# A mixed-attention kernel: another plan table, output tokens turned back in pairs, a separate bank for the fourth key chunk and two queues for the last outputs

## The chip, the cores and the metric

The kernel runs on one core of a Trainium2 chip. The core has a matrix engine (TensorE, PE in the profile, with its weight loads as PEld), a vector engine (VectorE, DVE), an engine for functions of one operand (ScalarE, ACT), a general one (GpSimd, POOL) and SyncE (SP), which here issues DMAs. Each engine works through its own list of instructions in order, and semaphores hold the lists together. On-chip data lies in SBUF (128 partitions) and matrix results in PSUM, whose eight banks hold 512 float32 per partition each.

The metric is the device time of one execution in microseconds, as the median of several runs.

## What is computed

Two attentions over the same input are mixed by a gate. A is full softmax attention over 2,048 tokens with 32 heads of 20 channels; B looks at eight earlier tokens, two apart. Everything is bf16 at the interfaces.

```python
x = A_x                                             # 1 x 2048 x 640
g = sigmoid((x * gate_w).sum(-1, keepdims=True))
# A: q, k, v = split(x @ A_wqkv); per head
a = softmax(q @ k.T * 20 ** -0.5) @ v               # 2048 x 2048 scores per head
a = concat_heads(a) @ A_wo
# B: the same with its own weights; for each token only the keys at pos - 0, 2, ..., 14
b = concat_heads(o_B) @ B_wo
return g * a + (1 - g) * b
```

Most of the work is A: 32 heads of 2,048 x 2,048 scores, each with an exponential.

## The kernel before

**Tiling.** Queries are cut into four columns of 512 tokens (`qc`), heads into eight quads of four (`q`). A pair is a group; the 32 groups run in the order of `GROUPS`. In a group there are 16 blocks of 128 keys times four heads, so 64 score blocks of 128 keys x 512 queries, and 2,048 in all. A head's score block is one matrix product of 32 rows of `kT` and `qT` (20 channels, a bound, padding), so four heads share the partitions.

**The main loop.** `next_tile` takes two or three score blocks as a tile. `qk` (L1508) computes them into one of two triple banks, `score[0]` and `score[1]`, in turn. `exp` (L1531) is one exponential on ACT over the tile, into one of five `ebuf`. `pv` (L1576) multiplies the results with the values `vA` and accumulates the four heads of a quad in `obank`. So the score matmuls of tile s wait until the exponential of tile s-2 has read its bank. The third bank of each triple (`side[1]`, `side[2]`) can instead serve other work; `side[0]` always does. Those three are the side banks.

**Rides.** With a tile of two, a third score block may ride on DVE: L1521 turns the scores into integers that read as powers of two, L797 adds three shifts, and `vS` (made by POOL, L789) holds weighted values, so that four products of such blocks approximate the exponential. This takes blocks off ACT.

**The side work.** All else (projections of Q, K and V, the gate, attention B, and the fold, which is the last product with both output weights) is written as generators. They ask for a side bank, for PE time up to a limit, or for DVE. All their matmuls go through `mm_group` (L558), which cuts weights into pieces of 32 columns. `filler` (L1597) puts matmuls without use into gaps of PE.

**The order.** It is all made when the program is built. A planner keeps a model of when each engine is free; at each tile it grants side work until the earlier exponential's planned end plus `SLACK`. The table `PLAN` sets 18 numbers (`SLACK`, what a ride may wait for, priorities, the filler threshold and so on) from given tiles on. The chip only follows the resulting lists.

**Normalising.** When a group is done, `gen_norm` turns `obank` by 32 x 32 blocks (L759), takes the reciprocal of the denominators (L763), multiplies them with the gate (L765) and the outputs with both (L770, on POOL; on DVE in the last group), and turns the bf16 result back (L772) into `oN[1]`. DMAs spread it into `oTd`, whose columns are tokens; the fold uses 32 tokens at a time as weights.

**Head.** The first key quad is projected in four chunks (`k_first`, L1247) which take `side[0]` and `obank` in turn; each is measured by DVE (L1261) and copied to `kT` by ACT (L1268). The first query projection goes to `side[1]`, is turned into absolute values (L1323), a bound is added to it (L1326), and DVE writes `qT[0]` (L1331).

**Tail.** `gen_prefold` and `gen_prefold2` compute the last query column's fold for all but the last quad. Then `tail` (L1057) adds the last quad's part, ACT (L1076) and DVE (L1070, L1079) copy the results to SBUF, and SP issues four DMAs of 128 rows (L1084).

Of the kernel before, what the change touches and what calls it, by code (L numbers as in the profile page):

```python
# [14 lines left out]
P = 128  # L15
# [35 lines left out]
    0: ((0.36, 0.81), 0.32, 2.5, 6.6, 0.49, -1.0, -0.1, 11.8, 7.0, 7.2, 0.52, 0.47, 4.4, 4.44, 0.0, 0.85, 2, 0.0),  # L51
    10: ((0.41, 0.67), 0.29, 2.5, 6.6, 0.49, -1.0, -0.32, 10.6, 6.7, 7.2, 0.52, 0.61, 4.4, 4.44, 0.0, 0.85, 2, 0.0),
    30: ((0.3, 0.64), 0.32, 2.5, 2.5, 0.49, -1.0, -0.1, 11.8, 7.0, 6.95, 0.47, 0.5, 4.97, 4.0, 0.0, 0.85, 2, 0.0),
    40: ((0.42, 0.67), 0.29, 2.5, 6.6, 0.49, -1.0, -0.32, 10.6, 6.7, 7.2, 0.52, 0.61, 4.4, 4.44, 0.0, 0.85, 2, 0),
    70: ((0.41, 0.67), 0.29, 2.5, 2.5, 0.83, -1.02, -0.32, 10.6, 5.5, 7.2, 0.42, 0.61, 5.71, 4.44, -0.04, 0.85, 3, 0.0),
    80: ((0.42, 0.67), 0.29, 5.5, 6.6, 0.49, -1.0, -0.32, 10.6, 6.7, 7.2, 0.52, 0.48, 4.4, 4.44, 0.12, 0.85, 2, 0),
    90: ((0.42, 0.67), 0.05, 2.5, 6.6, 0.49, -1.0, -0.32, 10.6, 6.7, 7.2, 0.52, 0.61, 4.4, 4.44, 0.0, 0.6, 2, 0),
    110: ((0.3, 0.64), 0.32, 2.5, 1.0, 0.49, -1.0, -0.1, 11.8, 7.0, 7.2, 0.4, 0.47, 4.77, 3.55, -0.02, 0.85, 2, 0.0),
    120: ((0.3, 0.61), 0.32, 2.5, 6.3, 0.49, -1.0, -0.1, 10.63, 7.0, 7.2, 0.4, 0.56, 4.29, 4.0, 0.0, 0.85, 2, 1),
    130: ((0.3, 0.61), 0.28, 2.5, 6.3, 0.62, -1.0, -0.1, 10.63, 7.0, 7.2, 0.39, 0.56, 4.29, 4.0, 0.0, 0.85, 2, -3),  # L60
    140: ((0.3, 0.61), 0.22, 2.5, 5.5, 0.4, -1.0, 0.01, 9.77, 7.0, 7.2, 0.33, 0.21, 4.29, 4.0, 0.0, 0.85, 2, 0.0),
    150: ((0.3, 0.64), 0.32, 2.5, 2.5, 0.49, -1.0, -0.35, 11.8, 7.0, 7.2, 0.52, 0.47, 4.4, 4.0, 0.1, 0.85, 2, 0.0),
    190: ((0.3, 0.64), 0.32, 1.0, 2.5, 0.49, -1.0, -0.1, 11.8, 7.0, 7.2, 0.55, 0.47, 4.56, 4.0, 0.0, 0.85, 2, 0.0),
    200: ((0.3, 0.64), 0.32, 1.0, 2.5, 0.49, -0.57, 0.17, 11.8, 7.0, 7.2, 0.55, 0.47, 4.56, 4.0, 0.04, 0.85, 2, 0.0),
    210: ((0.3, 0.64), 0.32, 2.5, 2.5, 0.49, 0.26, 0.1, 11.8, 4.5, 11.1, 0.56, 0.32, 4.97, 4.0, -0.25, 0.85, 2, -3),
    230: ((0.3, 0.64), 0.32, 2.5, 2.5, 0.49, 0.05, -0.54, 11.8, 6.7, 11.1, 0.56, 0.47, 5.29, 2.82, -0.48, 0.85, 2, -3),
    240: ((0.3, 0.64), 0.32, 1.0, 6.3, 0.49, -0.85, -0.1, 11.39, 6.7, 11.1, 0.56, 0.27, 4.97, 4.0, -0.25, 0.85, 2, -3),
    260: ((0.3, 0.64), 0.32, 1.0, 6.3, 0.49, -0.34, -0.1, 11.39, 6.7, 10.86, 0.56, 0.27, 4.97, 4.0, 0.08, 0.85, 2, -3),
    290: ((0.3, 0.64), 0.32, 1.0, 6.3, 0.49, -0.34, -0.1, 11.39, 4.5, 10.86, 0.56, 0.27, 4.97, 4.0, 0.08, 0.85, 2, -3),
    300: ((0.3, 0.64), 0.32, 1.0, 6.3, 0.49, -0.34, -0.1, 11.39, 4.5, 10.86, 0.56, 0.27, 6.29, 4.0, 0.05, 0.85, 2, -3),  # L70
    320: ((0.3, 0.64), 0.27, 1.0, 6.3, 0.49, -0.83, -0.1, 11.39, 4.5, 10.86, 0.69, 0.23, 5.37, 4.0, 0.05, 0.61, 2, -3),
    330: ((0.3, 0.64), 0.27, 1.0, 6.3, 0.49, -0.72, -0.1, 11.39, 4.5, 7.69, 0.69, 0.23, 5.37, 4.0, 0.05, 0.61, 2, -3),
    340: ((0.3, 0.64), 0.14, 1.0, 6.3, 0.49, -1.05, 0.17, 11.39, 6.7, 10.63, 0.3, 0.34, 5.37, 4.43, 0.05, 0.61, 2, -3),
    350: ((0.3, 0.64), 0.16, 1.0, 6.3, 0.49, -0.25, -0.1, 8.61, 6.7, 10.86, 0.56, 0.27, 4.97, 4.0, 0.08, 0.85, 2, -3),
    360: ((0.3, 0.64), 0.27, 1.0, 5.5, 0.7, -0.83, -0.1, 12.93, 4.5, 11.67, 0.69, 0.23, 5.37, 4.0, 0.05, 0.61, 2, -3),
    390: ((0.3, 0.64), 0.27, 1.0, 6.3, 0.7, -0.83, -0.1, 12.93, 7.0, 10.86, 0.69, 0.23, 5.37, 4.0, 0.2, 0.61, 2, -3),
    400: ((0.3, 0.64), 0.27, 1.0, 6.3, 0.7, -0.83, -0.1, 12.93, 7.0, 9.69, 0.69, 0.23, 5.37, 1.85, 0.2, 0.6, 2, -3),
    420: ((0.3, 0.64), 0.27, 1.0, 6.3, 0.7, -0.83, -0.07, 12.93, 4.5, 10.86, 0.5, 0.23, 5.37, 4.0, 0.1, 0.61, 2, -3),
    430: ((0.3, 0.64), 0.27, 1.0, 6.3, 0.7, -0.83, -0.07, 12.93, 6.2, 10.86, 0.5, 0.23, 5.37, 4.0, 0.1, 0.61, 2, -3),
    440: ((0.3, 0.64), 0.27, 1.0, 6.3, 0.7, -0.83, -0.07, 12.93, 4.5, 10.86, 0.5, 0.23, 5.64, 4.45, 0.1, 0.75, 2, -3),  # L80
    460: ((0.3, 0.64), 0.27, 1.0, 5.5, 0.8, -0.83, -0.07, 11.24, 4.5, 10.15, 0.5, 0.23, 5.12, 4.0, 0.1, 0.61, 2, -3),
    470: ((0.3, 0.62), 0.27, 1.0, 5.5, 0.8, -0.83, -0.03, 11.24, 4.5, 10.15, 0.5, 0.23, 5.12, 4.0, 0.2, 0.61, 2, 0),
    480: ((0.3, 0.62), 0.27, 1.0, 5.5, 0.8, -0.83, -0.03, 11.24, 4.5, 10.15, 0.5, 0.2, 5.12, 4.0, 0.2, 0.63, 2, 0),
    490: ((0.3, 0.64), 0.27, 1.0, 5.5, 0.16, -1.11, -0.07, 11.24, 4.5, 10.15, 0.5, 0.22, 5.12, 4.0, 0.1, 0.61, 2, -3),
    500: ((0.35, 0.7), 0.27, 1.0, 5.5, 0.8, -1.41, -0.07, 11.24, 4.5, 10.15, 0.5, 0.23, 5.12, 3.63, 0.0, 0.66, 2, 0),
    510: ((0.42, 0.67), 0.27, 1.0, 5.5, 0.8, -1.41, -0.07, 11.24, 4.5, 9.79, 0.5, 0.23, 5.12, 3.63, 0.0, 0.66, 2, 0),
    530: ((0.35, 0.7), 0.27, 1.0, 5.5, 1.18, -1.27, -0.07, 11.24, 4.5, 10.15, 0.5, 0.37, 5.12, 3.63, -0.18, 0.66, 2, -1.5),
    540: ((0.35, 0.7), 0.27, 1.0, 5.5, 1.18, -1.27, -0.07, 7.73, 4.5, 10.15, 0.5, 0.37, 5.12, 3.63, -0.08, 0.66, 2, -1.5),
    550: ((0.4, 0.81), 0.31, 1.0, 1.0, 1.22, -0.92, -0.07, 11.24, 4.5, 10.15, 0.5, 0.23, 5.12, 3.63, -0.18, 0.66, 2, -1.5),
    570: ((0.35, 0.7), 0.27, 1.0, 6.3, 1.18, -1.27, -0.07, 7.73, 4.5, 10.15, 0.5, 0.37, 5.12, 3.63, 0.06, 0.66, 2, -3),  # L90
    580: ((0.35, 0.7), 0.27, 1.0, 6.3, 1.18, -1.16, -0.07, 7.73, 4.5, 10.15, 0.53, 0.23, 5.12, 3.63, 0.06, 0.66, 2, -3),
    590: ((0.4, 0.59), 0.27, 1.0, 1.0, 1.14, -1.27, -0.07, 15.91, 5.5, 9.02, 0.53, 0.44, 5.12, 3.63, -0.18, 0.77, 2, -3),
    600: ((0.35, 0.7), 0.27, 1.0, 1.0, 1.18, -0.31, -0.07, 7.73, 4.5, 10.15, 0.49, 0.23, 5.12, 3.63, 0.12, 0.66, 1, 0),
    610: ((0.35, 0.7), 0.27, 1.0, 1.0, 1.18, -0.31, -0.07, 7.73, 4.5, 10.15, 0.57, 0.52, 5.12, 3.63, 0.12, 0.66, 1, 0),
    620: ((0.4, 0.75), 0.2, 5.5, 6.3, 1.18, -1.27, -0.12, 9.15, 6.7, 9.11, 0.46, 0.35, 4.77, 4.62, -0.12, 0.66, 2, -3),
    630: ((0.35, 0.7), 0.27, 2.5, 6.3, 1.18, -1.03, -0.07, 7, 6.2, 8.26, 0.53, 0.23, 6.21, 3.33, 0.01, 0.66, 2, -3),
    640: ((0.3, 0.64), 0.27, 2.5, 2.5, 0.49, -1.0, -0.1, 11.8, 7.0, 7.89, 0.52, 0.33, 4.4, 4.0, -0.43, 0.79, 1, 0.0),
    660: ((0.41, 0.72), 0.14, 6.6, 6.3, 1.18, -1.27, -0.08, 14.43, 4.5, 8.95, 0.5, 0.37, 4.72, 4.37, -0.12, 0.66, 2, 0),
    670: ((0.41, 0.72), 0.14, 2.5, 6.3, 1.18, -1.2, 0.05, 9.91, 4.5, 9.11, 0.69, 0.37, 4.72, 4.37, -0.12, 0.66, 2, 0),
    690: ((0.37, 0.63), 0.12, 2.5, 6.3, 1.4, -1.14, 0.33, 9.91, 5.5, 9.11, 0.5, 0.37, 4.72, 1.64, -0.12, 0.66, 2, -3),  # L100
    710: ((0.41, 0.72), 0.14, 2.5, 6.3, 1.18, -1.35, -0.08, 9.91, 4.5, 9.11, 0.5, 0.64, 4.57, 4.41, -0.12, 0.66, 2, 0),
# [220 lines left out]
def _build(ctx, nc, A_x, A_wqkv, A_wo, B_wqkv, B_wo, gate_w, out):  # L322
# [221 lines left out]
    def mm_group(b, mms, reads, cost, first=True, last=True, per=1):  # L544
# [3 lines left out]
        for i0 in range(0, n, per):  # L548
# [3 lines left out]
            def fn(e, i0=i0, i1=i1):  # L552
                ins = None
                for i in range(i0, i1):
                    o, l, r = mms[i]
                    for j in range(0, l.shape[-1], 32):
                        k = min(j + 32, l.shape[-1])
                        ins = e.matmul(o[j:k, :], l[:, j:k], r, start=(first and i == 0),  # L558
                                       stop=(last and i == n - 1), skip_group_check=True)
                return ins  # L560
# [196 lines left out]
    def gen_norm(g):  # L757
        qc, q = GROUPS[g]
        T("dve", dvc(512), lambda e: e.transpose(oTt[:, :], obank[:, :]), reads=["obank"], writes=["oTt"])  # L759
        while not done.get(("gate", qc)):  # L760
# [4 lines left out]
        T(en, c1, lambda e: e.tensor_tensor(rcp[:, :], rcp[:, :], gA[qc % 2][:, :], ALU.mult),  # L765
          reads=["rcp", ("gA", qc % 2)], writes=["rcp"])
        ib = _ap(rcp, 0, [[1, 16], [0, 32]])
        oo = oN[0][:, :].rearrange("p (b c) -> p b c", c=32)
        ii = _ap(oTt, 0, [[32, 16], [1, 32]])
        T(en, c2, lambda e: e.tensor_tensor(oo, ii, ib, ALU.mult), reads=["rcp", "oTt"], writes=["oN0"])  # L770
        yield ("dve", DVE_AHEAD, max(sch.ready("oN0"), sch.free("oN1")))
# [999 lines left out]
```

## Time and profile before

The median of three runs is 840.44 us (840.35 to 840.74). The profiled execution took 841.16 us.

| | before |
|---|---|
| profiled execution | 841.16 us |
| span of its instructions | 839.4 us |
| first exponential starts | 20.3 us |
| last exponential starts | 826.2 us |
| PE score<-qT,kT (L1508), 2,048 matmuls | 284.5 us busy, 384 ns each |
| DVE rides (L1521), 311 | 210.0 us busy, 685 ns each |
| DVE shifts (L797), 231 of 2,048 and 3 of 1,536 elements | 713 and 552 ns each |
| granted TensorE clock, mean | 0.998 of full speed |

In a row of the profile the tile written stands left of the arrow and what is read right of it; then come the shapes, the count, the total busy time, the mean duration in ns, and the idle time of the engine just before these instructions with what ended it. A timeline row gives start and length in us of a run of like instructions. Durations of matmuls and of ACT overlap those of their successors.

### The profile page before, as it was taken

To read this page: it belongs to the slowest core of one execution; us is meant where nothing else is said; L and a number is where in the kernel's file an instruction comes from. 1 tells how busy PE (TensorE), PEld (TensorE's weight loads), DVE (VectorE), ACT (ScalarE), POOL (GpSimd) and SP (SyncE) were. 2 spreads that over 40 slices of the span, in tenths; PEclk is the share of its full clock that TensorE was granted. 3 is DMA by queue.
4 is the path that set the end of the run, shared out by engine and by line. 5 is a ranking of instruction groups with operands and counts; after the bars stand their busy time and mean duration, and the time that the engine had idled before them with its cause. 6 is when DMAs were issued, how large, how long until landed. Compare 5 with 4: busy or idle time off the path is not lost.

```text
span 839.4 us, 29881 instructions
## 1 busy us (share of the span) xinstructions
PE 791.8 (94%) x12798; PEld 294.1 (35%) x12798; DVE 675.7 (81%) x1183; ACT 808.2 (96%) x747; POOL 129.9 (15%) x177
## 2 busy tenths in 40 slices
PE   8999999999999999999998898999899999999997
PEld 5432332333333333433333333333343333342223
DVE  6577887879887888887888888898898878888763
ACT  4999999999999999999999999999999999999994
POOL 5040111620110110111110111111011111102100
PEclk9999999999999999999999999999999999999999
DMA  9002121200111101010100111010010010101000
GB/s 312 29 15 46 40 44 38 69 17 18 34 30 36 30 16 27 16 32 25 24 19 25 35 20 36 12 43 23 25 32 21 21 36 21 30 7 26 17 5 34
DMA packets 45017, 29.16 MB, mean 35 GB/s; under 512 B 27205, under 2 KB 43685, under 8 KB 44885
## 3 DMA queue, kind: packets, MB, share of 16 engines
q1 hardware_dynamic: 44884, 27.25, 12.5%
q8 instruction: 101, 1.65, 0.8%
q14 instruction: 32, 0.25, 0.1%
HBM read 11.94 MB, written 2.62 MB: 17 GB/s over the span
## 4 chain that ended last, share of the span: by engine, by line
PE 43%; ACT 39%; issue 12%; DVE 4%; SPq 1%; DMA 0%; DVEq 0%; ACTq 0%
ACT ebuf L1531 38%; PE score L1508 13%; PE side L558 10%; PE obank L1576 10%; PE score L558 5%; PE obank L1597 2%; DVE uD L1521 1%; DVE eD L797 1%; PE score L1597 1%; SPq L705 1%; PE side L1597 1%; PE score L1224 1%; PE obank L461 1%; ACT eB L914 0%; PE side L885 0%
## 5 line engine op out<-in xcount | busy, mean ns | idle before, releaser
L1531 ACT ACTIVATE ebuf<-score 128x1024 bf16<-128x1024 f32 (+1 forms) x715 | 796.9, 1259 | 9.6 <-PE score L1508 7.6
L1508 PE MATMUL score<-qT,kT 32*128 32x512 bf16 x2048 | 284.5, 384 | 31.0 <-ACT ebuf L1531 22.5
L1521 DVE TENSOR_SCALAR uD<-score 128x512 int16<-128x512 f32 x311 | 210.0, 685 | 56.0 <-PE score L1508 52.4
L1508 PEld LDWEIGHTS score<-qT,kT 32*128 32x128 bf16 x2048 | 72.0, 91 | 272.8 <-ACT ebuf L1531 125.5
L797 DVE TENSOR_SCALAR eD<-uD 128x2048 int16<-128x2048 int16 (+1 forms) x234 | 161.0, 711 | 3.8 <-PE obank L1576 2.5
L1576 PE MATMUL obank<-ebuf,vA 128*21 128x512 bf16 x1737 | 158.9, 385 | 2.8 <-ACT ebuf L1531 1.4
L558 PE MATMUL side<-xT,kvw 128*32 128x256 bf16 (+1 forms) x2580 | 106.0, 282 | 2.2 <-DVE dst L662 0.9
L789 POOL TENSOR_TENSOR vS<-vA,vw 128x252 bf16<-128x252 bf16 x78 | 53.4, 689 | 275.7 <-PE obank L1576 234.3
L1576 PE MATMUL obank<-eD,vS 128*21 128x512 bf16 x933 | 81.8, 379 | 0.0
L558 PEld LDWEIGHTS side<-xT,kvw 128*32 128x32 bf16 x2580 | 60.7, 96 | 37.4 <-issue 19.9
L765 POOL TENSOR_TENSOR rcp<-rcp,gA 128x16 f32<-128x16 f32 x31 | 9.8, 316 | 368.1 <-DVE rcp L763 368.1
L1576 PEld LDWEIGHTS obank<-ebuf,vA 128*21 128x21 bf16 x1737 | 37.6, 89 | 83.2 <-issue 69.5
L970 DVE TENSOR_TENSOR stage<-qkvB,repB 128x1280 bf16<-128x1280 bf16 x64 | 52.2, 839 | 0.1
L853 DVE CAST qkvB<-side 128x512 bf16<-128x512 f32 (+1 forms) x72 | 42.1, 593 | 11.3 <-PE side L558 10.7
L869 DVE TENSOR_TENSOR stage<-qkvB 128x1280 bf16<-128x1280 bf16 x64 | 50.4, 826 | 0.2
L558 PE MATMUL side<-stage,ident 128*32 128x512 bf16 (+1 forms) x768 | 49.1, 346 | 0.7 <-DVE dst L662 0.5
L1597 PE MATMUL obank<-xT,zero 128*32 128x512 bf16 x560 | 43.6, 382 | 0.0
L770 POOL TENSOR_TENSOR oN<-oTt,rcp 128x512 bf16<-128x512 f32 x31 | 32.5, 1050 | 2.4
L759 DVE STREAM_TRANSPOSE oTt<-obank 128x512 f32<-128x512 f32 x32 | 22.8, 712 | 11.1 <-PE obank L1576 11.0
L1576 PE MATMUL obank<-uD,vA 128*21 128x512 bf16 x311 | 30.3, 379 | 0.0
L772 DVE STREAM_TRANSPOSE oN<-oN 128x512 bf16<-128x512 bf16 x32 | 22.5, 705 | 9.3 <-POOL oN L770 9.0
L1576 PEld LDWEIGHTS obank<-eD,vS 128*21 128x21 bf16 x933 | 23.0, 91 | 15.9 <-issue 2.3
(161 smaller groups left out, 577.5 us busy)
## 6 DMA issues: line engine op xcount, KB each, us to landing
repB<-eB SPq DMA_DIRECT2D x128, 32.0 KB
WqP<-in_A_wqkv_dram SPq DMA_DIRECT2D x16, 160.0 KB
stage<-in_B_wqkv_dram SPq DMA_DIRECT2D x1, 2400.0 KB
oTd<-oN SPq DMA_DIRECT2D x108, 20.0 KB
qT<-dst SPq DMA_DIRECT2D x104, 20.0 KB
out_dram<-outsb SPq DMA_DIRECT2D x12, 160.0 KB
kvw<-in_A_wqkv_dram SPq DMA_DIRECT2D x2, 800.0 KB
oTd<-in_A_x_dram SPq DMA_DIRECT2D x2, 640.0 KB
```

Of the source, the lines that this page charges most:

```text
L558: ins = e.matmul(o[j:k, :], l[:, j:k], r, start=(first and i == 0), stop=(last and i == n - 1), skip_group_check=True)
L770: T(en, c2, lambda e: e.tensor_tensor(oo, ii, ib, ALU.mult), reads=["rcp", "oTt"], writes=["oN0"])
L789: T("pool", 0.7, lambda e: e.tensor_tensor(vS[:, d % 2, :, :], _ap(vA, (kb * NQ + q) * 4 * DV, [[0, K - 1], [1, 4 * DV]]), _ap(vw, 0, [[1, ...
L797: T("dve", 0.11 + 0.1334 * n, lambda e, k=k, sl=sl: e.tensor_scalar(eD[:, sl % NS, 0:512 * n].bitcast(I16), uD[d % 2][:, 0:512 * n].bitcas ...
L853: t = TB(dvc(n * TOK), lambda e, o=o, i=i: e.tensor_copy(o, i), reads=[("side", b)], writes=[key])
L869: TB(dvc(CN * TOK, 2), lambda e, w=w, ks=ks: e.tensor_tensor(prodB(w), qB[:, :, :], ks, ALU.mult), reads=["qB", "kB"], writes=[("prod", w) ...
L970: TB(dvc(CN * TOK, 2), lambda e, w=w, vs=vs, rr=rr: e.tensor_tensor(prodB(w), vs, rr, ALU.mult), reads=["vB", ("repB", w4 % NR)], writes=[ ...
L1508: ins = e.matmul(o, kT[32 * j:32 * j + 32, q, kb * P:(kb + 1) * P], qT[g % NQT][32 * j:32 * j + 32, :], start=True, stop=True)
L1521: t = T("dve", 0.69, lambda e: e.tensor_scalar(uD[d % 2][:, 512 * i:512 * (i + 1)].bitcast(I16), side[x], UOFF, 0.0, op0=ALU.add, op1=ALU. ...
L1531: exps[s] = T("act", actc(512 * n), lambda e: e.activation(ebuf[s % NE][:, 0:512 * n], score[s % 2][:, 0:512 * n], ACTF.Exp, scale=LN2 / S ...
L1576: ins = e.matmul(obank[32 * j:32 * j + DV, :], v, src, start=(kb == 0), stop=(last and k >= len(lst) - 4), skip_group_check=True)
L1597: ins = e.matmul(o[32 * j:32 * j + 32, :], w[:, 32 * j:32 * j + 32] if best else w[:, :], xT[:, 0, 0:512], start=bool(best), stop=bool(bes ...
```

## The change

There are five edits.

1. `PLAN` is another table, with other numbers and other tiles from which they hold. The order of nearly all side work, rides and tiles moves with it.
2. In `gen_norm` the multiply writes its result so that tokens t and t + 64 of each block of 128 lie side by side, and the second transpose treats such a pair as one 32-bit word: 256 words instead of 512 elements.
3. The folds read the weights of `oTd` and `oN[1]` with a step of two (`paired`), which undoes the pairing; `mm_group` takes a function for such weights, and the tail's matmuls are cut into pieces of 32 columns.
4. In the head, the fourth key chunk goes to `side[1]` instead of `obank`, and the first query projection to `obank` instead of `side[1]`.
5. The last four output DMAs are issued in the order 2, 3, 0, 1; ACT issues the first two of these, SP the others.

The code of the main loop, the rides, attention B and the planner's own costs stay.

```diff
 PLAN = {
-    0: ((0.36, 0.81), 0.32, 2.5, 6.6, 0.49, -1.0, -0.1, 11.8, 7.0, 7.2, 0.52, 0.47, 4.4, 4.44, 0.0, 0.85, 2, 0.0),
...
-    710: ((0.41, 0.72), 0.14, 2.5, 6.3, 1.18, -1.35, -0.08, 9.91, 4.5, 9.11, 0.5, 0.64, 4.57, 4.41, -0.12, 0.66, 2, 0),
+    0: ((0.34, 0.64), 0.37, 6.3, 2.5, 0.51, -1.0, -0.1, 11.8, 4.5, 7.2, 0.52, 0.47, 4.4, 1.86, 0.0, 0.85, 2, 0.0),
...
+    700: ((0.42, 0.48), 0.32, 6.3, 5.5, 0.76, -0.49, -0.43, 10.79, 5.5, 10.35, 0.65, 0.53, 6.0, 4.64, -0.33, 0.63, 2, -3),
 }
...
-                    for j in range(0, l.shape[-1], 32):
-                        k = min(j + 32, l.shape[-1])
-                        ins = e.matmul(o[j:k, :], l[:, j:k], r, start=(first and i == 0),
+                    n_ = P if callable(l) else l.shape[-1]
+                    for j in range(0, n_, 32):
+                        k = min(j + 32, n_)
+                        ins = e.matmul(o[j:k, :], l(j) if callable(l) else l[:, j:k], r, start=(first and i == 0),
...
-        ib = _ap(rcp, 0, [[1, 16], [0, 32]])
-        oo = oN[0][:, :].rearrange("p (b c) -> p b c", c=32)
-        ii = _ap(oTt, 0, [[32, 16], [1, 32]])
+        ib = _ap(rcp, 0, [[4, 4], [2, 2], [1, 2], [0, 32]])
+        oo = _ap(oN[0], 0, [[128, 4], [1, 2], [64, 2], [2, 32]])
+        ii = _ap(oTt, 0, [[128, 4], [64, 2], [32, 2], [1, 32]])
         T(en, c2, lambda e: e.tensor_tensor(oo, ii, ib, ALU.mult), reads=["rcp", "oTt"], writes=["oN0"])
...
-        T("dve", dvc(512), lambda e: e.transpose(oN[1][:, :], oN[0][:, :]), reads=["oN0"], writes=["oN1"])
+        T("dve", dvc(256), lambda e: e.transpose(oN[1][:, :].bitcast(FP32), oN[0][:, :].bitcast(FP32)), reads=["oN0"], writes=["oN1"])
...
+    def paired(of, blk):
+        at = lambda j: blk * P + 2 * (j % 64) + j // 64
+        return lambda j: of(slice(at(j), at(j) + 63, 2))
...
-            return [(o, oN[1][:, tok], woA_l[:, c0:c1])]
+            return [(o, paired(lambda c: oN[1][:, c], blk), woA_l[:, c0:c1])]
...
-                (o, oTd[:, qc % 2, f, tok], woA_d[:, f, c0:c1]) for f in range(CN)]
+                (o, paired(lambda c, f=f: oTd[:, qc % 2, f, c], blk), woA_d[:, f, c0:c1]) for f in range(CN)]
...
-                    ins = e.matmul(o, l, r, start=not accum, stop=True, skip_group_check=True)
+                    for j in range(0, P, 32):
+                        ins = e.matmul(o[j:j + 32, :], l(j), r, start=not accum, stop=True, skip_group_check=True)
...
-        for blk in range(4):
+        for blk in (2, 3, 0, 1):
             row = (QCN - 1) * 512 + blk * P
-            T("sp", 2.0, lambda e, blk=blk, row=row: e.dma_start(out_v[row:row + P, :], tout[blk]),
+            T("act" if blk > 1 else "sp", 2.0, lambda e, blk=blk, row=row: e.dma_start(out_v[row:row + P, :], tout[blk]),
...
-    kbank = lambda tcc: (side[0], ("side", 0)) if tcc % 2 == 0 else (obank, "obank")
+    kbank = lambda tcc: ((side[0], ("side", 0)), (obank, "obank"), (side[0], ("side", 0)), (side[1], ("side", 1)))[tcc]
...
-    T("pe", 1.07, proj5(side[1][:, :], lambda c: WqP[:, c, :], None, 0), reads=WQ + XT(0), writes=[("side", 1)])
+    T("pe", 1.07, proj5(obank[:, :], lambda c: WqP[:, c, :], None, 0), reads=WQ + XT(0), writes=["obank"])
...
-    t = T("dve", dvc(512), lambda e: e.tensor_scalar(qT[0][:, :], side[1][:, :], OCT, offs[:, 0:1], op0=ALU.mult, op1=ALU.add),
-          reads=[("side", 1), "offs", ("qTz", 0)], writes=[("qT", 0)])
+    t = T("dve", dvc(512), lambda e: e.tensor_scalar(qT[0][:, :], obank[:, :], OCT, offs[:, 0:1], op0=ALU.mult, op1=ALU.add),
+          reads=["obank", "offs", ("qTz", 0)], writes=[("qT", 0)])
```

In the built order, the change has 479 exponentials of two blocks and 255 of three (406 and 308 before, and one of one block in both), 324 rides (311), 2,048 score matmuls in both, 3,020 matmuls of L1576's kind (2,981) and 748 fillers (1,008). The key maximum, the bound and the copies of the head and the planner's notes of when banks come free follow the banks.

## The prediction

> **What bounds the kernel now.** I read the share of each engine first, then the windows by stage, then the costliest groups by form, then two stretches of the timeline of ACT and the timeline of both ends. The span is 839.4 us; the profiled execution took 841.16 us, 0.72 above the median of 840.44. My sum is a difference, so I subtract it from both.
>
> ```profile
> PE 791.8 (94%) x12798; PEld 294.1 (35%) x12798; DVE 675.7 (81%) x1183; ACT 808.2 (96%) x747; POOL 129.9 (15%) x177
> ...
> ACT ebuf L1531 38%; PE score L1508 13%; PE side L558 10%; PE obank L1576 10%; PE score L558 5%; PE obank L1597 2%; DVE uD L1521 1%; DVE eD L797 1%; PE score L1597 1%; SPq L705 1%; PE side L1597 1%; PE score L1224 1%; PE obank L461 1%; ACT eB L914 0%; PE side L885 0%
> ```
>
> ```profile
> L1531 ACT ACTIVATE ebuf<-score 128x1536 bf16<-128x1536 f32 x308 | 432.1, 1501 | 3.8 <-PE score L1508 3.0 <-ACT ebuf L1531 0.3
> L1531 ACT ACTIVATE ebuf<-score 128x1024 bf16<-128x1024 f32 x406 | 398.0, 1076 | 5.7 <-PE score L1508 4.6
> ```
>
> ACT is never idle for long (9.6 us before its exponentials); PE's 94% holds fillers and modelled ends, and the chain hops between ACT's exponential and PE because a score bank is refilled only once its exponential is read. So the **rate of the exponentials** between 20.3 and 826.8 us sets the middle. The busy means overlap their successors, so the price of one is its start-to-start time:
>
> ```profile
> 139.33 7.51 ACT L1531 ACTIVATE ebuf<-score 128x1024 bf16<-128x1024 f32 x8
> ...
> 729.88 6.84 ACT L1531 ACTIVATE ebuf<-score 128x1536 bf16<-128x1536 f32 x5
> ```
>
> (6.84 - 1.50)/4 = 1.335 us for a tile of three; (7.51 - 1.08)/7 = 0.92 for a tile of two, whose starts there lie 0.904 apart (the last took 1.18). Over the whole trace the shortest steps are 0.904 and 1.330. Then 406 x 0.904 + 308 x 1.330 = 776.7 us, and with ACT's small work in between the starts leave about 24 us more than this floor: 1.3 behind the first tile, 16.9 behind tiles of two (0.042 each), 6.0 behind tiles of three (0.019 each). These 24 us are stalls too short to show as idle rows.
>
> **The plan table.** The order of instructions after the change has 479 tiles of two, 255 of three (one of one stays): 324 instead of 311 of the 2,048 score blocks ride on DVE, and fewer tiles find a third bank free.
> - Floor of ACT: 479 x 0.904 + 255 x 1.330 = 772.2, against 776.7: **-4.5**.
> - Stalls. What follows a tile is set by the PE work put between its score matmuls and the next ones. I priced that work from the rows (four 32-column matmuls of 512 in 0.215 us, as the fold's 80 in 4.76 below), sorted before's tiles by size and work, and took each class's mean stall. Tiles of two with 0.8 to 1.0 us of work stalled 0.155 us on average; there are 18 of them before and 49 after. Those with 0.6 to 0.8 (0.078) fall from 111 to 87; tiles of three with over 1.0 us (0.044) from 83 to 57. Summed over all classes: 22.9 before, 25.1 after (+2.2). Sorted by the sizes of neighbouring tiles alone: 24.3 (+1.4). I take **+1.8**.
> - DVE: 13 more of L1521 x 0.685 = 8.9; L797 243 x 0.713 against 231 x 0.713 + 3 x 0.552 = +6.9. POOL: 3 more vS x 0.69. PE: 39 more output matmuls = 10 sets of four x 0.215 = 2 us, and 260 fewer fillers = 65 sets = 14 us less. DVE is idle about 160 us, so its work is hidden by the exponentials unless a ride frees a bank late, and this is inside the classes above. Were PE's clock to fall with the fillers it would cost much, but it was granted 1.00 in every window from 20 to 826 us, and priced real work plus fillers is 616 us before, 608 after.
>
> **Pairs of tokens.** The multiply (L770) writes bf16 two elements apart, so two tokens share a 32-bit word; the second transpose turns 256 words instead of 512 elements.
>
> ```profile
> L759 DVE STREAM_TRANSPOSE oTt<-obank 128x512 f32<-128x512 f32 x32 | 22.8, 712 | 11.1 <-PE obank L1576 11.0
> ...
> L772 DVE STREAM_TRANSPOSE oN<-oN 128x512 bf16<-128x512 bf16 x32 | 22.5, 705 | 9.3 <-POOL oN L770 9.0
> L770 POOL TENSOR_TENSOR oN<-oTt,rcp 128x512 bf16<-128x512 f32 x31 | 32.5, 1050 | 2.4
> ```
>
> 512 elements take 0.71 us in either type, so the price is per element; L853's casts take 0.682 for 512 and 0.416 for 256, so 256 words should take 0.71 - 0.27 = 0.44. That saves 0.27 x 32 = 8.5 us of DVE, which pays more than half of the added 15.8 (net +7.3), but no wall time by itself. The multiply's step of two is in no row. Bounds: nothing, or half as long again (+0.5 x 31 = 16 us of POOL); nobody is near to waiting for POOL (15% busy; its results feed folds a column of queries later), so I take 0, at worst +1 through DVE waiting for a port. The last group's multiply is on DVE (0.69), 2.4 us ahead of its user.
>
> The folds' weights are read with a step of two: 640 loads of oTd and 32 of oN1. Rows near: a load of 32 contiguous columns takes 0.096 us and twenty follow each other in 0.48, 0.020 each; the gate's weights with step 0 (L558, gwT) also take 0.095. Here a rule bears: the Trainium skill, SBUF — State Buffer, SBUF: two separate sides, says that a 16-byte line gives full bandwidth as long as two accesses or more hit it, so bf16 may step by up to 8. By it the cost is 0; by the distrust that no row has step two, a load twice as long costs 0.02 x 336 of the narrow folds = 6.9 us of PE (wide ones give 0.054 per matmul and hide it), about 1 of it in the tail. I take 0.
>
> **Head.** K's fourth chunk gets its own bank instead of obank, and the query projection goes to obank.
>
> ```profile
> 14.63 0.68 ACT L1268 ACTIVATE kT<-obank,onesrow 128x512 bf16<-128x512 f32 x1
> ...
> 15.43 0.77 PEld L1247 LDWEIGHTS obank<-xT,kvw 128*128 128x128 bf16 x5 [1.17 <-DVE xT L1240]
> 15.46 1.24 PE L1247 MATMUL obank<-xT,kvw 128*128 128x512 bf16 x5 [0.70 <-ACT kT L1268]
> ```
>
> The fourth chunk waits until ACT has read obank (15.31). Without it the last xT piece is late next: ACT's ends at 14.73, so the start is 14.87, 0.59 earlier. The reduce (16.73), the eB product, qabs and qT follow one another on DVE; L1318 ends at 16.18 and caps the gain at **0.55**. Query matmuls end early enough, and the third block of the first tile waits only for ACT's read of chunk three, over a microsecond earlier. Also 12 instead of 20 matmuls stand last ahead of the second score tile (twenty took 0.68): **-0.27**.
>
> **Tail.** After the last exponential (826.81) PE does:
>
> ```profile
> 827.11 0.22 PE obank L1576 x4
> 827.32 0.50 PE side L558 x28
> 827.82 4.76 PE score L558 x80
> 832.59 1.21 PE score L1057 x8
> ```
>
> The new order leaves 56 narrow matmuls there instead of 28: **+0.5**. The eight wide matmuls of L1057 become 32 of 32 columns, 16 x 0.054 + 16 x 0.02 = 1.2: 0. DVE's norm chain (827.37 to 830.13) is shadowed by PE until 832.5.
>
> ```profile
> 834.43 0.68 DVE L1079 TENSOR_TENSOR stage<-score,qabs 128x512 bf16<-128x512 f32 x1
> 834.54 2.22 SPq L1084 DMA_DIRECT2D out_dram<-stage  x4
> ```
>
> SP issues rows 0 and 1 at 834.54 and 835.14 as DVE ends them, then rows 2 and 3 at 835.61 and 836.42, though ACT had them ready at 834.26. In the change ACT issues 2 and 3 itself from about 834.3, and SP ends its second at 835.5 instead of 836.75: -1.25 if landing (2.6 us after the last issue) stays. The rule against it: the Trainium skill, DMA: Bandwidth & Descriptors, Issuing engines are not separate DMA queues: a second issuer saves only sequencer time, the same engines move the bytes. Row: that sequencer time is 1.25 us here; rule: the saving has this ceiling, and the floor is 0 if the four transfers (0.65 MB) then queue. ACT's first DMA is in no row. I take **-1.2**.
>
> **Sum**: -4.5 + 1.8 - 0.55 - 0.27 + 0.5 - 1.2 = -4.2. From 841.16 this gives 837.0; from the median 836.2. I forecast **836.5**, own range 834 to 838.6.
>
> **Rivals.**
> - *The fuller tiles of two stall harder* (slower). A tile of two has the least room: four sets (0.87) and a score set (0.22) exceed its 0.904 by 0.18, and with the mode change seen as 0.23 of issue idle by 0.4. Before, most such slots followed a tile of three, which gave room; after, 16 of 49 stand between two tiles of two with an overrun of 0.15 us or more, against 4 before, and those four stalled 0.22. If the 49 stall 0.30 instead of 0.155: +7.1, 843.3. It turns to slower at 0.155 + 4.2/49 = 0.24. For it: the class mean rests on 18 tiles. Against it: 0.24 is above even those four.
> - *Strided weights are twice as slow*: +1.4 in the tail's narrow loads and L1057, and up to 5 in the six earlier folds, half of it on the path: 836.5 + 3.9 = 840.4, no change. Against it: the step-0 row.
> - *The new order stalls less than its classes say*: the plan's allowance of PE work past an exponential's end falls from 0.30 to about 0.28 and later 0.20, fillers go. If stalls fall by 2 instead of rising by 1.8: 832.7.
>
> **Numbers.** Forecast 0.55, harder stalls 0.21, slow weights 0.13, fewer stalls 0.11. What this kernel can tell is 0.2%, 1.7 us: faster means under 838.8, slower over 842.1. The forecast gives 0.54 of faster, the weights 0.03, fewer stalls 0.11: 0.68; harder stalls give slower 0.18, weights 0.02: 0.20; the rest 0.12. The range 832.0 to 842.8 leaves half of the harder stalls and a little at the low end outside.
>
> **What would show it.** First exponential at 19.5 to 19.8 us; exponential rows x479 and x255; the transpose at 0.44 us; oTd loads still at 0.096; four output issues ending by 835.7 relative to this tail; ACT's starts between first and last exponential some 3 us closer together. A mean stall behind tiles of two above 0.05 us, or loads near 0.12, would make me wrong.

## The result, and the profile after

The changed kernel takes 837.22 us (median of four runs, 836.29 to 837.48), the kernel before beside it 840.59. The ratio is 0.9955 with a 95% interval of 0.9938 to 0.9973: 3.8 us faster, between 2.3 and 5.2. The forecast was 836.5. The profiled execution took 837.19 us, its span is 835.4 against 839.4.

The page of the changed kernel, its engines and the costliest group:

```profile
PE 789.3 (94%) x12599; PEld 289.9 (35%) x12601; DVE 683.7 (82%) x1205; ACT 803.9 (96%) x767; POOL 138.7 (17%) x180
...
L1538 ACT ACTIVATE ebuf<-score 128x1024 bf16<-128x1024 f32 (+1 forms) x735 | 792.6, 1237 | 11.6 <-PE score L1515 9.7
```

ACT is still the engine that is never idle for long, at the same 96%. DVE carries 8.0 us more although its transposes shrank. By form, from the groups of the same trace, with the edited instructions of the pairs:

```profile
L1538 ACT ACTIVATE ebuf<-score 128x1024 bf16<-128x1024 f32 x479 | 463.4, 1082 | 6.4 <-PE score L1515 5.0
L1538 ACT ACTIVATE ebuf<-score 128x1536 bf16<-128x1536 f32 x255 | 359.2, 1530 | 5.1 <-PE score L1515 4.4 <-ACT ebuf L1538 0.2
...
L770 POOL TENSOR_TENSOR oN<-oTt,rcp 128x512 bf16<-128x512 f32 x31 | 33.0, 1065 | 2.4
...
L772 DVE STREAM_TRANSPOSE oN<-oN 128x256 f32<-128x256 f32 x32 | 13.9, 436 | 4.8 <-POOL oN L770 4.6
L557 PEld LDWEIGHTS side<-woA_d,oTd 128*32 128x32 bf16 x560 | 10.8, 96 | 6.9 <-issue 4.3
```

The transpose of 256 words takes 0.436 us (0.705 for 512 elements before), the multiply with a step of two 1.065 (1.050), and a weight load with a step of two 0.096, as one without.

The spans differ by 3.97 us. The starts of the exponentials and the ends of the span split the difference (ACT's small work between the exponentials, 5.0 us, and the last exponential, 0.6, are alike in both and stand in no row):

| term | before | after | difference | forecast |
|---|---|---|---|---|
| first exponential starts | 20.31 | 19.62 | -0.69 | -0.55 |
| time behind the first tile over its floor | 1.35 | 1.09 | -0.27 | -0.27 |
| floor of the exponentials (0.904 and 1.330 each) | 776.7 | 772.2 | -4.5 | -4.5 |
| stalls behind all other tiles | 22.9 | 25.3 | +2.5 | +1.8 |
| last exponential's end to the tail's matmuls | 5.78 | 6.33 | +0.55 | +0.5 |
| tail's matmuls to the end of the last DMA issue | 4.16 | 2.94 | -1.22 | -1.25 |
| last issue to the end of the span | 2.62 | 2.32 | -0.30 | 0 |

(The forecast took the last two rows together as -1.2.)

Part of the stalls is not the order's. In the profile of the changed kernel the granted clock fell to half from 456.15 to 459.57 us. In a row of the windows stand the window, its length, the busy times of PE, PEld, DVE, ACT and POOL, the granted clock, the DMA share and GB/s:

```profile
456.00:459.60 3.60, 3.60 (x46) 1.30 (x43) 1.60 (x4) 2.96 (x3) 2.29 (x3) 0.53 0.12 27
```

The two tiles of three that ran there stall 0.79 and 0.49 us, 1.3 together. At the prediction's rate the 16 output matmuls behind the first are 0.86 us of work against a tile of 1.33, so at full clock hardly any stall would be expected there (an estimate). Without these two tiles the stalls differ by some +1.2 instead of +2.5. The profile before has no such fall between its first and last exponential.

The end of the chain of waits of the changed kernel, start and length in us:

```profile
823.22 0.61 ACT ebuf L1538
823.82 0.04 issue
823.87 0.40 PE obank L1583 x4
824.26 1.12 PE side L557 x56
825.38 4.76 PE score L557 x80
830.14 1.23 PE score L1063 x32
831.37 0.02 issue
831.39 0.69 DVE stage L1085
832.09 0.60 DVEq L263
```

The 56 narrow matmuls (28 before) are the longer way to 830.14; the eighty wide ones last 4.76 as before. The timeline after that shows both issuers:

```profile
831.43 0.86 ACTq L1090 DMA_DIRECT2D out_dram<-stage  x2
832.00 0.68 DVE L1085 TENSOR_TENSOR stage<-score,qabs 128x512 bf16<-128x512 f32 x1
832.11 0.96 SPq L1090 DMA_DIRECT2D out_dram<-stage  x2
```

ACT's two issues lie beside DVE's last sums, and SP ends 0.40 us after the last sum, where it ended 1.65 after it before.

### The profile page after: what moved, and what is told of

Its sections match the earlier page's. It is cut to its first block, busy times and chain, and to the rows that moved or that the text cites. A ratio compares the mean times of both kernels' runs of the same rounds, so it can differ in the third digit from the quotient of the medians.

```text
span 835.4 us, 29602 instructions
## 1 busy us (share of the span) xinstructions
PE 789.3 (94%) x12599; PEld 289.9 (35%) x12601; DVE 683.7 (82%) x1205; ACT 803.9 (96%) x767; POOL 138.7 (17%) x180
## 3 DMA queue, kind: packets, MB, share of 16 engines
HBM read 11.94 MB, written 2.62 MB: 17 GB/s over the span
## 4 chain that ended last, share of the span: by engine, by line
PE 54%; ACT 30%; issue 10%; DVE 5%; DVEq 0%; ACTq 0%
ACT ebuf L1538 30%; PE score L1515 17%; PE obank L1583 13%; PE side L557 13%; PE score L557 5%; PE obank L1604 2%; DVE uD L1528 1%; PE side L1604 1%; DVE eD L797 1%; PE obank L459 1%; PE score L1230 1%; PE side L885 1%; DVE stage L869 0%; PE score L1604 0%; DVE stage L970 0%
## 5 line engine op out<-in xcount | busy, mean ns | idle before, releaser
L1515 PE MATMUL score<-qT,kT 32*128 32x512 bf16 x2048 | 291.9, 384 | 31.6 <-ACT ebuf L1538 20.6
L1528 DVE TENSOR_SCALAR uD<-score 128x512 int16<-128x512 f32 x324 | 217.2, 683 | 38.4 <-PE score L1515 36.1
L797 DVE TENSOR_SCALAR eD<-uD 128x2048 int16<-128x2048 int16 x243 | 168.1, 722 | 7.9 <-PE obank L1583 7.2
L1515 PEld LDWEIGHTS score<-qT,kT 32*128 32x128 bf16 x2048 | 75.1, 91 | 282.7 <-ACT ebuf L1538 137.6
L1583 PE MATMUL obank<-ebuf,vA 128*21 128x512 bf16 x1724 | 161.3, 385 | 2.2 <-ACT ebuf L1538 1.8
L789 POOL TENSOR_TENSOR vS<-vA,vw 128x252 bf16<-128x252 bf16 x81 | 61.0, 757 | 291.5 <-PE obank L1583 256.3
L557 PE MATMUL side<-xT,kvw 128*32 128x256 bf16 (+1 forms) x2530 | 103.0, 281 | 3.1 <-DVE qkvB L853 1.4
L1604 PE MATMUL obank<-xT,zero 128*32 128x512 bf16 x444 | 37.9, 385 | 0.0
L557 PE MATMUL side<-woA_d,oTd 128*32 128x128 bf16 (+1 forms) x580 | 28.8, 293 | 0.0
```

Source lines behind the costliest of these rows:

```text
L557: ins = e.matmul(o[j:k, :], l(j) if callable(l) else l[:, j:k], r, start=(first and i == 0), stop=(last and i == n - 1), skip_group_check= ...
L789: T("pool", 0.7, lambda e: e.tensor_tensor(vS[:, d % 2, :, :], _ap(vA, (kb * NQ + q) * 4 * DV, [[0, K - 1], [1, 4 * DV]]), _ap(vw, 0, [[1, ...
L797: T("dve", 0.11 + 0.1334 * n, lambda e, k=k, sl=sl: e.tensor_scalar(eD[:, sl % NS, 0:512 * n].bitcast(I16), uD[d % 2][:, 0:512 * n].bitcas ...
L1515: ins = e.matmul(o, kT[32 * j:32 * j + 32, q, kb * P:(kb + 1) * P], qT[g % NQT][32 * j:32 * j + 32, :], start=True, stop=True)
L1528: t = T("dve", 0.69, lambda e: e.tensor_scalar(uD[d % 2][:, 512 * i:512 * (i + 1)].bitcast(I16), side[x], UOFF, 0.0, op0=ALU.add, op1=ALU. ...
L1583: ins = e.matmul(obank[32 * j:32 * j + DV, :], v, src, start=(kb == 0), stop=(last and k >= len(lst) - 4), skip_group_check=True)
```

## The experiments

Four kernels separate the parts. Since the planner reorders everything when a time early in its model changes, each variant keeps an order as it was: behind the head, the planner's clocks are set to the values of the kernel whose order is kept, and the price that it assumes for the transpose stays. So each list of instructions differs from the original's only in the edited ones. The kernel before ran beside them with a median of 841.49 us. Turning x means the product with `ident` (L1224 before), four sets of 20 matmuls in the head.

| kernel | median us | ratio to before, 95% interval | first exponential | the same, counted from the fourth turning of x | stalls, without the first tile | last exponential's end to span's end |
|---|---|---|---|---|---|---|
| before (first profile) | 840.44 | | 20.31 | 7.92 | 22.9 | 12.56 |
| after (first profile) | 837.22 | 0.9955, 0.9938 to 0.9973 | 19.62 | 7.94 | 25.3 | 11.58 |
| plan alone | 838.75 | 0.9967, 0.9956 to 0.9978 | 19.36 | 7.91 | 27.4 | 12.66 |
| head alone | 840.68 | 0.9990, 0.9981 to 0.9999 | 19.64 | 7.52 | 23.0 | 12.37 |
| pairs alone | 841.94 | 1.0006, 0.9997 to 1.0014 | 19.98 | 7.92 | 25.4 | 12.54 |
| queues alone | 840.13 | 0.9977, 0.9969 to 0.9986 | 20.19 | 7.92 | 23.0 | 10.99 |

**The plan alone.** The changed kernel, with the pairs, the head and the queues taken back (three cuts of the edit):

```diff
-            return [(o, paired(lambda c: oN[1][:, c], blk), woA_l[:, c0:c1])]
+            return [(o, oN[1][:, tok], woA_l[:, c0:c1])]
...
-        for blk in (2, 3, 0, 1):
+        for blk in range(4):
...
-    T("pe", 1.07, proj5(obank[:, :], lambda c: WqP[:, c, :], None, 0), reads=WQ + XT(0), writes=["obank"])
+    T("pe", 1.07, proj5(side[1][:, :], lambda c: WqP[:, c, :], None, 0), reads=WQ + XT(0), writes=[("side", 1)])
```

> The changed kernel's order of all instructions, but head, pairs and output queues as before. Theory (the plan gives its floor and takes stalls): floor of the exponentials -4.5 us, stalls behind them about +2.5, second tile -0.3, 28 more narrow matmuls at the end +0.5: about -1.8 us against before. Rival (the gain comes from head and tail, the plan gives nothing): within 0.5 of before. Rival (the plan gives nearly all): -3 or more.

The ratio gives -2.8 us, between -1.9 and -3.7. So the plan gives the largest part of the gain, and the rival that gives it nothing is out. The theory's -1.8 lies just outside the interval, and the -3 of the rival that gives it nearly all lies inside; the clocks at the end of this section bring the measured gain nearer to the theory. Its profiled execution, at 840.16, is 1.4 above its median, and the reason stands in its timeline. PE, which works in order, waits 1.95 us at a fold's first matmul for the DMA of the last normalised outputs, and the next exponential stalls for 1.4:

```profile
812.01 0.13 PEld L556 LDWEIGHTS side<-woBp,oB 128*32 128x32 bf16 x4 [2.21 <-issue]
812.04 0.40 PE L556 MATMUL side<-woBp,oB 128*32 128x512 bf16 x4 [1.95 <-DMA oTd<-oN]
...
812.87 2.96 ACT L1542 ACTIVATE ebuf<-score 128x1536 bf16<-128x1536 f32 x2 [1.29 <-PE score L1519]
```

In the changed kernel the same matmul started at 810.11, although SP ended the last issue of that DMA at nearly the same time (808.88 here, 808.79 there). With this tile and the two that it delayed (0.35 and 0.19) back at the changed kernel's values, the plan alone has 25.5 us of stalls, against 25.3 in the whole change. Both hold a fall of the clock at the same place of the order: here it lasts from 455.67 to 459.08, with stalls of 0.69 and 0.60. Why the transfer landed so much later here is not shown.

The narrow matmuls cost what was expected: the tail's matmuls start 6.33 us after the last exponential's end, as in the whole change. That the end is only 0.1 longer than before comes from SP's four issues (1.95 us instead of 2.22) and the landing after them (2.43 instead of 2.62), which no edit of this kernel touches.

**The head alone.**

```diff
-    kbank = lambda tcc: (side[0], ("side", 0)) if tcc % 2 == 0 else (obank, "obank")
+    kbank = lambda tcc: ((side[0], ("side", 0)), (obank, "obank"), (side[0], ("side", 0)), (side[1], ("side", 1)))[tcc]
```

> The kernel before, in its order, with the fourth key chunk in side[1] and the first query projection in obank. Theory: first exponential 0.6 to 0.7 us earlier, and the span shorter by as much, because ACT sets the middle from there on. Rival: the lead is lost again in the first tiles (the second tile waits for PE): first exponential earlier, span within 0.2.

The ratio gives -0.8 us (0.1 to 1.6), so it is a gain, and the middle keeps it: the stalls stay at 23.0, tile by tile as before. But the first exponential is not 0.6 us earlier by this edit. The four kernels without it start it 7.91 to 7.92 us after the fourth turning of x, and that turning itself starts anywhere from 11.45 to 12.39 (why, the last section says). With the edit it starts at 19.62 and 19.64, wherever the turning was (11.68 and 12.12). So it has run into something fixed. The timeline of the changed kernel shows what:

```profile
12.11 3.99 POOL L1302 COPY kT<-ones 128x1024 f32<-128x1024 f32 x4
...
14.10 1.24 PE L1253 MATMUL score<-xT,kvw 128*128 128x512 bf16 x5
...
14.99 1.15 DVE L1324 TENSOR_SCALAR eB<-eB,kmx 128x128 bf16<-128x128 bf16 x1
...
16.06 0.68 DVE L1267 TENSOR_REDUCE kmx<-score 128x1 f32<-128x512 f32 x1
```

The fourth chunk's matmuls begin at 14.10, 1.36 earlier than before, and end at 15.34. Its maximum on DVE still waits, for the small product ahead of it in DVE's list, which takes 1.15 us here. Before, it took 0.47, and DVE was idle behind it until the bank was filled:

```profile
15.71 0.47 DVE L1318 TENSOR_SCALAR eB<-eB,kmx 128x128 bf16<-128x128 bf16 x1
16.73 0.69 DVE L1261 TENSOR_REDUCE kmx<-obank 128x1 f32<-128x512 f32 x1 [0.56 <-PE obank L1247]
```

POOL's four fills of `kT` end at 16.10. In all six profiles this product ends 0.04 to 0.06 us after the end of one of POOL's fills: in five of them after the last (16.16 against 16.11 with the head alone), and with the plan alone after the third (15.14 against 15.09):

```profile
14.76 0.38 DVE L1317 TENSOR_SCALAR eB<-eB,kmx 128x128 bf16<-128x128 bf16 x1
```

So the product, not the bank, holds the start of the attention once the bank is free. The Trainium skill, SBUF — State Buffer, SBUF: two separate sides, has a mechanism that fits: some DVE modes share a pair of ports with GpSimd, as a lock held for a whole instruction. No run here moved the product or the fills, so the lock is the reading that the six coincidences support, not one that was tried.

**The pairs alone.**

```diff
-        T("dve", dvc(512), lambda e: e.transpose(oN[1][:, :], oN[0][:, :]), reads=["oN0"], writes=["oN1"])
+        T("dve", dvc(512), lambda e: e.transpose(oN[1][:, :].bitcast(FP32), oN[0][:, :].bitcast(FP32)), reads=["oN0"], writes=["oN1"])
```

> The kernel before, in its order, with tokens in pairs and weights read with a step of two, and the tail's matmuls in 32 columns. Theory: 8.6 us less of DVE for the transposes, loads of oTd at 0.096 us as before, span within 0.5 us of before. Rival (a freer DVE shortens the stalls): -1.5 us or more. Rival (strided loads or the strided multiply cost): +1 us or more, seen in the loads of oTd or in POOL's multiply.

The ratio is 1.0006, and its interval holds 1: no change that can be told, as expected. The groups of its trace exclude the costs:

```profile
L773 DVE STREAM_TRANSPOSE oN<-oN 128x256 f32<-128x256 f32 x32 | 14.0, 438 | 9.3 <-POOL oN L771 9.1
L559 PEld LDWEIGHTS side<-woA_d,oTd 128*32 128x32 bf16 x520 | 10.1, 96 | 6.4 <-issue 3.2
```

Its profile has 2.5 us more of stalls than before, but not from the pairs: two events carry it, 1.06 behind one tile at 607 us and 0.74 behind the third tile at 24 us. At 607 us PE took 2.32 us for 20 projection matmuls, and the windows say why:

```profile
600.00:607.00 7.00, 5.82 (x97) 1.88 (x94) 5.08 (x9) 6.93 (x10) 0.00 (x0) 1.00 0.16 42
607.00:609.40 2.40, 2.22 (x20) 0.70 (x20) 0.99 (x3) 2.20 (x2) 0.00 (x0) 0.50 0.20 51
```

The clock was at half: its record has 0.50 from 607.01 to 610.43, 3.4 us, of which the second window is the first part. At 24 us PE stood still for 0.73 us in the middle of a group of matmuls, with no wait that the profile shows:

```profile
24.41 0.45 PE L559 MATMUL score<-kvw,xT 128*32 128x320 bf16 x7 [0.73 <-issue]
```

With the two taken off, 23.6 us remain, and what still lies over the 22.9 of before is mostly the tiles right behind these two.

**The queues alone.**

```diff
-        for blk in range(4):
+        for blk in (2, 3, 0, 1):
...
-            T("sp", 2.0, lambda e, blk=blk, row=row: e.dma_start(out_v[row:row + P, :], tout[blk]),
+            T("act" if blk > 1 else "sp", 2.0, lambda e, blk=blk, row=row: e.dma_start(out_v[row:row + P, :], tout[blk]),
```

> The kernel before, in its order, with output rows 2 and 3 issued by ACT and rows 0 and 1 by SP. Theory: last issue ends 1.25 us earlier and the landing is as long or up to 0.3 shorter: span -1.2 to -1.5. Rival (the four transfers queue on the same engines): landing longer by what the issue gains, span within 0.4 of before.

```profile
833.86 0.86 ACTq L1084 DMA_DIRECT2D out_dram<-stage  x2
834.44 0.68 DVE L1079 TENSOR_TENSOR stage<-score,qabs 128x512 bf16<-128x512 f32 x1
834.54 0.96 SPq L1084 DMA_DIRECT2D out_dram<-stage  x2
```

The last issue ends at 835.51, 1.24 earlier than before, and the span ends 2.30 after it instead of 2.62. The end is 1.57 us shorter, at an equal end of the last exponential (826.82 and 826.81). The ratio says 1.9 (1.2 to 2.6), a little more than the trace. The transfers do not queue: the landing became shorter, not longer. But not all of the 0.3 is the edit's: the four profiles in which SP issues all four outputs have landings of 2.43 to 2.62 us, the two with two issuers 2.30 and 2.32.

By their ratios the four parts sum to -0.60%, 5.0 us; the whole gave 0.45% (0.27 to 0.62). So they add up within the interval.

The executions of these kernels did not have the same clock, though. The mean granted clock was 0.997 or less in 14 of the 32 of the kernel before, in 4 of 10 with the plan alone, 1 of 11 with the head alone, 8 of 11 with the pairs alone and 1 of 11 with the queues alone. All eight executions of the kernel before above 842.5 us are among the 14, and none at 0.998 or more took over 841.67. Where the clock was lower in each is not known, as one execution of each kernel was profiled. Among those at 0.998 or more the medians are 841.12 before, and 839.28, 840.65, 841.19 and 839.97 for the four parts: -1.8, -0.5, +0.1 and -1.2, together -3.4. These groups are small (18, 6, 10, 3 and 10), but they lie nearer to the whole's -3.8, and the plan's part lies on the theory's -1.8.

All three edits on the old order in one kernel, and the changed kernel a second time beside its parts, were not run.

## Why the prediction was right

It was right in its sum and in most of its terms. Two terms hold luck: the head's, whose size came from a clock that rose earlier in the profile after, and the stalls', which hold a fall of the clock. The first took 0.7 off the profile's span that the edit did not give, the second added 1.3; together they moved the sum by 0.6.

- **Floor of ACT, -4.5.** Right. The shortest steps of the changed kernel are again 0.903 and 1.330, and the plan table alone carries the largest part of the gain.
- **Stalls, +1.8.** Right in sign; 0.7 short of the +2.5, and 0.6 above the +1.2 that is left without the fall of the clock, which is no term of the sum. By classes, reckoned as in the prediction: behind tiles of two with 0.8 to 1.0 us of work, 49 tiles stall 0.120 each, where 0.155 was taken (5.9 instead of 7.6); those with 0.6 to 0.8 sum to 5.9 (6.9 taken). The misjudged class is tiles of two with over 1.0 us of work, seven of them, taken at 0.8 us in sum. They sum to 3.2, 1.1 of it behind one tile at 54 us, with 12 gate matmuls and five sets of output matmuls between its score set and the next one.
- **Pairs, 0.** Right, with the forecast's 0.44 for the transpose. A load with a step of two took 0.096 us, so the row for a contiguous load held, and with it the rule on lines that the prediction cites.
- **Head, -0.55.** The cap that was named held: with the edit the product ends at 16.14 and 16.16, where the prediction had "L1318 ends at 16.18 and caps the gain". What it missed is that this end goes with one of POOL's fills and does not move with the turnings of x, so the edit gives the more the later the turning is: at the 12.39 of before some 0.68 (12.39 + 7.92 - 19.63, an estimate). Counted from the fourth turning it gave 0.40 alone, and nothing in the profiled execution of the whole change. There, the 0.69 came from the first turning of x: its successor started 2.25 us after it instead of 2.95, because PE reached its full rate 1.5 us earlier (last section). No edit is known to do that: with the old head, the same turning would have given 19.60 (11.68 + 7.92, an estimate) where 19.62 was measured. So the agreement with -0.55 is luck.
- **Second tile, -0.27, and narrow matmuls, +0.5.** Right (0.27, 0.55).
- **Queues, -1.2.** Issuing gave 1.22, the landing another 0.3, of which 0.1 to 0.3 is beyond what it is with SP alone. The rule weighed against it, that a second issuer saves only its own issue time, names exactly the part that was gained.

Of the rivals, harder stalls needed 0.24 behind each of the 49 tiles and got 0.120; slow weights needed longer loads and got 0.096; fewer stalls (-2) are excluded by +2.5, and by the +1.2 without the fall of the clock.

What is open: what sets the moment at which PE reaches its full rate, and what makes the clock fall in the middle; whether the small product is held by POOL's port, which running it on ACT would tell; and whether cutting the output matmuls in the 49 full slots would remove their 5.9 us. None of these was tried.

## What to carry to other kernels

Where one engine's stream sets the time and a planner reorders everything, price a new order as a floor, the count of its instructions times their shortest start-to-start time, plus the stalls of the old trace by class of slot; here the stalls carried over within 1 us. Before taking a wait off the path, look whether the next instruction there ends by its own length or together with another engine's instruction: in the second case the gain stops at a fixed time. The last transfers of a kernel are worth spreading over two issuers when their issues, and not the bytes, are in line.

## What the runs showed of the hardware that was not expected

- **Stalls are a property of the order.** With the same order, the head-alone and queues-alone kernels repeat the stalls of before tile by tile (23.0 and 23.0 us against 22.9; the largest difference at any tile is 0.15 us). What differs between the profiled executions are single events: above, a late transfer (1.4 us), falls of the clock (1.3 and 1.1) and a standstill of PE (0.7).
- **The clock can halve for a moment.** It fell to 0.50 for 3.4 us in three of the six profiled executions: the changed kernel's and the plan alone's at the same place of the order, and the pairs alone's at 607 us. The mean over the span hides it: 0.998 in the profile after, with the fall, and 0.998 before, without it. In the 3.4 us ahead of each fall PE was busy for 2.2 us. That is little for this kernel, but not the cause by itself: in the plan alone 2.1 us of work in the 3.4 from 281.6 on was followed by none. Whether the new order, with its fewer fillers, has more falls is not shown.
- **PE reaches its full rate at another moment in each execution.** The distance from the first to the second turning of x was 2.02 to 2.95 us in the six profiles; later ones lie about 2.2 apart to within 0.02. The count of matmuls from 5 to 6 us, the first number in brackets, shows it (before, after, plan alone):

```profile
5.00:6.00 1.00, 1.00 (x11) 0.96 (x11) 0.36 (x6) 0.00 (x0) 0.00 (x0) 1.00 1.06 371
5.00:6.00 1.00, 1.00 (x14) 0.98 (x14) 0.36 (x6) 0.00 (x0) 0.00 (x0) 1.00 1.06 379
5.00:6.00 1.00, 1.00 (x18) 1.00 (x18) 0.36 (x6) 0.00 (x0) 0.00 (x0) 1.00 1.07 373
```

The twenty matmuls start some 0.107 us apart in the trace before, to the last; in the changed kernel the step goes from 0.107 to 0.056 behind the sixth, and with the plan alone behind the first. The windows read 1.00 all the same, because the record of the granted clock begins only at that moment: at 7.09, 5.59 and 5.11 us in these three, and at 6.53, 6.27 and 6.79 with head, pairs and queues alone. The first matmul started at 1.22 us in all six. A start that differs by 0.9 us between two single profiles can be this alone.
